# Expert rows of a routed network read in 256-byte pieces and turned by VectorE, in place of gathers turned by TensorE

## The chip, the cores and the metric

The kernel runs on one core of a Trainium2 chip. A core has five engines, each with an instruction queue of its own that is worked off in order: TensorE (PE; its weight loads are shown as PEld), VectorE (DVE), ScalarE (ACT), GpSimd (POOL) and SyncE (SP), which only issues transfers. All transfers run on the same 16 DMA engines. Matrix products land in PSUM, in banks that must be emptied before they are used again; everything else lies in SBUF (128 partitions) or in DRAM.

The metric is the time of one execution on the device, in microseconds. A few runs are made and their median is given; one more execution is recorded by the profiler.

## What is computed

A normalised linear attention, and then a layer of experts in which each token goes to one expert:

```python
kv  = einsum('bhsd,bhse->bhde', k, v)          # 8 batches, 8 heads, 576 tokens, 64 wide
out = einsum('bhsd,bhde->bhse', q, kv)
x   = out / sqrt(mean(out*out) + 1e-6) * g_norm  # rows: 4608 tokens x 512
...
expert = argmax(x @ w_gate)                    # one of 8
gate_w = softmax(x @ w_gate)[expert]
for e in range(8):
    h = relu(x[expert == e] @ w1[e])           # 512 -> 1024
    out[expert == e] = gate_w * (h @ w2[e])    # 1024 -> 512
```

The inputs q, k and v have 9.4 MB each and the expert weights 33.6 MB, all float32.

## The kernel before

**Attention.** A loop over b = 0 to 8 interleaves two things. For batch b it does the products k·v (`kv_mm`), the transposes of q (`t_mm`, a TensorE product with the identity, copied out by ACT) and `fold_mm`, which joins kv with the gate weights; `x_copy` brings the result to SBUF as `kvx`, one half by ACT and one half by VectorE. For the batch before, it runs four or five *tiles* of 128 tokens: `tile_step` multiplies q with kvx (`o_mm`, PSUM tag "O"), scales and casts the tile of before (`o_x`) and sums squares (`o_red`); `o_nrm` forms the root. The tiles are numbered (j, t), j = 0 to 3, t = 0 to 8. `load(b + 2, u)` is issued by SP as soon as the buffers of batch b are read, so loads run two batches ahead.

**Routing.** When some tiles are done (`chunks`: 9, 9, 3+6, 3+3+3), `route` is put on a list of jobs; `job()` is called twice a tile and runs it to its next `yield`. It finds each token's expert (`ohb`), counts with small TensorE products (`rps`) which row each token gets, and scatters the finished rows with 36 indirect transfers from POOL (line 743) into the DRAM array `x_slots`: 4608 rows for each of the 8 experts, a row being 512 float16, the gate's factor and the token's number (1032 bytes). The rows are built in `xrow`, with four buffers of three tiles each.

**Experts.** A row of work is a `Group`: three of 3 tiles (experts 0 to 2, whose first 384 rows are declared final once j = 0 to 2 are routed, `early_rows`), three of 2 tiles (the rest of experts 0 to 2), five of 5 tiles (experts 3 to 7). An expert has 640 slots; what is over goes to one more group of one tile (`SpillGroup`, with weights chosen at run time) and then to a loop of a count known only on the device (`LoopGroup`; with this input it has no round). For each group:

- `fetch` gathers the rows by indirect transfers of POOL, one for 128 rows (line 291), into a ring of three buffers `xl`. Slots that hold no row are left out by an index out of bounds; the ring was zeroed at the start.
- `xpose` turns each tile with four TensorE products with the identity into PSUM (`xps`, line 325), and VectorE writes it to `xsT` with the factor g_norm (line 328).
- `stage1(f)`, f = 0 to 7, is the first product (line 345, `hp`), with ACT's relu to `hT` (line 353).
- `stage2(k)` is the second product for 128 rows (line 361, `yp`), scaled by the gate on VectorE (line 366, `y`) and scattered to the output by POOL (line 369), with token numbers from `slot_ids`.

A generator, `ffn`, emits this a step at a time; `unit()` takes a step. The first steps are taken inside the last round of attention (b = 8, two after each tile from n = 3 on), one after each routing job, and the rest after it. The transposes of the next group are emitted between the stage 2 tiles of the present one, and the fetch of group r+2 at f = 0 of group r (the three early ones right after `early_rows`).

**Weights.** `w_load` (SP, lines 206 and 210) brings 512 KB into one of four staging buffers, `w_cast` (VectorE, line 220) turns it to float16; `w_step` does both, and is called from b = 6 on.

**Order.** The instructions of each engine run in the order in which the code emits them (`manual_schedule`). Waits between engines and between accesses to the same memory, `x_slots` and the output among it, are added by the framework: a reader of rows waits for the scatters emitted before it, a scatter for the readers emitted before it. The loop behind the experts stands outside this block: its count is read at line 850 by every engine, and its header (line 854) makes the engines wait for each other.

## Time and profile before

| | us |
|---|---|
| median of 3 runs (351.76 to 354.26) | 353.55 |
| the profiled execution's own time | 330.94 |
| its span, first to last instruction | 329.2 |
| TensorE busy | 269.0 |
| VectorE busy | 183.4 |
| GpSimd busy | 137.6 |
| ScalarE busy | 119.9 |

The profiled execution was 22.6 us shorter than the median of the runs; its mean granted TensorE clock was 0.903.

The costliest groups of instructions that the text below speaks of (line, engine, operation, output from inputs, how often, then busy us and mean ns of one, then idle us of the engine before them and what ended it):

```profile
L345 PE MATMUL hp<-xsT,w1e 128*128 128x320 f16 (+2 forms) x512 | 76.6, 306 | 7.2 <-DVE xsT L328 6.3
L361 PE MATMUL yp<-w2e,hT 128*128 128x512 f16 x320 | 74.1, 379 | 0.3 <-DVE y L366 0.3
...
L743 POOL DMA_INDIRECT x_slots<-xrow,posi x36 | 35.7, 991 | 40.5 <-DVE xrow L739 15.5
...
L291 POOL DMA_INDIRECT xl<-x_slots,idxa x31 | 32.4, 1046 | 11.7 <-issue 7.0
...
L328 DVE TENSOR_SCALAR xsT<-xps,g 128x512 f16<-128x512 f16 x41 | 19.2, 477 | 12.9 <-PE xps L325 12.7
```

In the timeline the last attention product ends at 148.6 us, the first expert product starts at 153.1, TensorE runs without larger gaps from 167.4, and its last product ends at 320.0. The scatters into `x_slots` run from 56.6 to 170.1, the nine early gathers from 139.8 to 152.2.

### The profile page before, as it was taken

What the parts mean: (1) busy time and instruction counts of PE and PEld (TensorE: products, weight loads), DVE (VectorE), ACT (ScalarE), POOL (GpSimd) and SP (SyncE); (2) the same over time, 40 slices, a digit from 0 to 9 for tenths busy, and PEclk for the clock granted to TensorE, in tenths of its full rate; (3) what the DMA queues carried; (4) which work ended last, traced back from release to release, by engine and by line L of the source; (5) the groups of instructions that cost most, each with busy time, mean ns of one, the idle gap of its engine ahead of it and who ended that gap; (6) DMA issues with size and microseconds to landing.
All of it is one profiled execution on the core that took longest, in us unless ns stands there. A gap on an engine that the chain in (4) does not pass through costs nothing.

```text
span 329.2 us, 7247 instructions
## 1 busy us (share of the span) xinstructions
PE 269.0 (82%) x2759; PEld 189.3 (58%) x2759; DVE 183.4 (56%) x433; ACT 119.9 (36%) x316; POOL 137.6 (42%) x147
## 2 busy tenths in 40 slices
PE   0699897689766977564979996989999999997980
PEld 0587776577656866462535563657565665645630
DVE  6205566346745368889184678344657658375040
ACT  1136564436543445322322431326142240602600
POOL 9100001720076004384675462777477656052041
PEclk9999997959995589555999998999999999999996
DMA  6999999997897016799589894667799999983021
GB/s 158 334 368 367 369 368 367 381 282 216 246 323 295 18 67 167 250 323 324 201 260 372 295 322 121 214 214 251 250 339 358 351 397 279 408 284 130 0 99 55
DMA packets 45395, 85.79 MB, mean 261 GB/s; under 512 B 6188, under 2 KB 22829, under 8 KB 45360
## 3 DMA queue, kind: packets, MB, share of 16 engines
q1 hardware_dynamic: 36736, 66.07, 59.9%
q0 software_dynamic: 6976, 18.96, 15.6%
q10 hardware_dynamic: 1648, 0.29, 0.5%
q8 instruction: 22, 0.36, 0.4%
q14 instruction: 13, 0.11, 0.1%
HBM read 71.77 MB, written 15.50 MB: 265 GB/s over the span
## 4 chain that ended last, share of the span: by engine, by line
PE 26%; issue 11%; DMA 9%; POOL 7%; DVE 5%; POOLq 1%; ACT 0%; DVEq 0%; ACTq 0%
PE hp L345 13%; PE yp L361 11%; DMA out_dram<-y,d_id 7%; POOL out_dram L369 4%; POOL xl L291 2%; DMA xl<-x_slots,idxe 2%; PE xps L325 1%; DVE y L366 1%; DMA x_slots<-xrow,posi 1%; POOL x_slots L743 1%; DVE w1e L220 1%; DVE xsT L328 0%; POOLq L888 0%; POOLq L854 0%; DVE w2e L220 0%
## 5 line engine op out<-in xcount | busy, mean ns | idle before, releaser
L353 ACT ACTIVATE hT<-hp 128x320 f16<-128x320 f32 (+3 forms) x136 | 53.6, 426 | 106.5 <-PE hp L345 105.9
L345 PE MATMUL hp<-xsT,w1e 128*128 128x320 f16 (+2 forms) x512 | 76.6, 306 | 7.2 <-DVE xsT L328 6.3
L361 PE MATMUL yp<-w2e,hT 128*128 128x512 f16 x320 | 74.1, 379 | 0.3 <-DVE y L366 0.3
L369 POOL DMA_INDIRECT out_dram<-y,idv x40 | 44.6, 1115 | 60.3 <-DVE y L366 49.3
L345 PEld LDWEIGHTS <-w1e 128*128 128x128 f16 x512 | 51.0, 100 | 32.1 <-issue 11.7
L651 PE MATMUL ops<-kvx,qT 64*128 64x72 f32 (+1 forms) x640 | 48.0, 310 | 10.5 <-DVE lhat L680 9.6
L743 POOL DMA_INDIRECT x_slots<-xrow,posi x36 | 35.7, 991 | 40.5 <-DVE xrow L739 15.5
L651 PEld LDWEIGHTS ops<-kvx,qT 64*128 64x128 f32 (+1 forms) x640 | 42.3, 215 | 15.0 <-issue 9.3
L361 PEld LDWEIGHTS <-hT 128*128 128x128 f16 x328 | 30.8, 98 | 31.6 <-issue 0.4
L366 DVE TENSOR_SCALAR y<-yp,xl 128x512 f32<-128x512 f32 x40 | 30.0, 750 | 33.6 <-PE yp L361 29.9
L664 DVE TENSOR_REDUCE ms<-sq 128x8 f32<-128x512 f32 x36 | 24.6, 685 | 25.1 <-ACT sq L660 25.0
L291 POOL DMA_INDIRECT xl<-x_slots,idxa x31 | 32.4, 1046 | 11.7 <-issue 7.0
L594 PE MATMUL kvps<-mk,mv 128*64 128x64 f32 x640 | 28.7, 258 | 9.4 <-DMA mv<-in_v_dram 9.1
L676 DVE TENSOR_TENSOR xrow<-ops,rs 128x512 f16<-128x512 f32 x36 | 24.7, 686 | 18.0 <-DMA x_slots<-xrow,posi 9.3
L660 ACT ACTIVATE sq<-ops 128x512 f32<-128x512 f32 x36 | 21.5, 598 | 31.9 <-PE ops L651 31.5
L594 PEld LDWEIGHTS kvps<-mk,mv 128*64 128x64 f32 x640 | 26.0, 168 | 11.8 <-issue 10.3
L710 POOL COPY xrow<-tokc 128x3 int32<-128x3 int32 x12 | 3.0, 253 | 64.3 <-DVE xrow L676 64.2
L582 PE MATMUL tps<-ctile,mq 128*128 128x128 f32 x144 | 26.9, 320 | 3.5 <-ACT qT L583 1.9
L220 DVE CAST w2e<-wst 128x1024 f16<-128x1024 f32 x32 | 22.3, 704 | 11.4 <-DMA wst<-in_moe_w_dram 11.4
L583 ACT COPY qT<-tps 128x384 f32<-128x384 f32 x48 | 21.9, 473 | 14.4 <-PE tps L582 14.4
L328 DVE TENSOR_SCALAR xsT<-xps,g 128x512 f16<-128x512 f16 x41 | 19.2, 477 | 12.9 <-PE xps L325 12.7
L220 DVE CAST w1e<-wst 128x1024 f16<-128x1024 f32 x32 | 21.6, 688 | 4.5 <-DMA wst<-in_moe_w_dram 4.5
(99 smaller groups left out, 184.1 us busy)
## 6 DMA issues: line engine op xcount, KB each, us to landing
wst<-in_moe_w_dram SPq DMA_DIRECT2D x64, 512.0 KB, 5.8
mq<-in_q_dram SPq DMA_DIRECT2D x16, 576.0 KB, 7.8
mk<-in_k_dram SPq DMA_DIRECT2D x16, 320.0 KB, 7.5
mv<-in_v_dram SPq DMA_DIRECT2D x16, 320.0 KB, 7.3
mk<-in_k_dram SPq DMA_DIRECT2D x16, 256.0 KB, 7.9
mv<-in_v_dram SPq DMA_DIRECT2D x16, 256.0 KB, 7.1
wsts<-in_moe_w_dram SPq DMA_DIRECT2D x8, 512.0 KB, 5.9
out_dram<-y,idv POOLq DMA_INDIRECT x40, 4.9
```

Of the source, the lines that this page charges most:

```text
L220: engine.tensor_copy(dst, st)
L291: nc.gpsimd.indirect_dma_start(out=self.xl[:, k, :], out_offset=None, in_=xs.ap(), in_offset=IndirectOffsetOnAxis(ap=idx[:, self.e, self.k ...
L345: nc.tensor.matmul(hp, self.w()[0][:, kk, f * 128 : (f + 1) * 128], self.xsT[:, kk, s : s + self.step], start=(kk == 0), stop=(kk == 3),)
L353: nc.scalar.activation(self.hT[:, f, s : s + self.step], hp, ACTF.Relu)
L361: nc.tensor.matmul(yp, self.hT[:, f, k * 128 : (k + 1) * 128], self.w()[1][:, f, :], start=(f == 0), stop=(f == 7),)
L366: nc.vector.tensor_scalar(y, yp, self.xl[:, k, D : D + 2].bitcast(F32), None, op0=ALU.mult)
L369: nc.gpsimd.indirect_dma_start(out=self.views(k), out_offset=IndirectOffsetOnAxis(ap=self.ids[:, k : k + 1], axis=0), in_=y, in_offset=Non ...
L582: nc.tensor.transpose(ps[:, c, :], src[:, 128 * m : 128 * m + 128], cv["ident"])
L594: nc.tensor.matmul(kvps[b][64 * y : 64 * y + 64, 2 * u + a, :], main["v", b, u][:, 2 * y + a, c, :], main["k", b, u][:, 2 * y + a, c, :], ...
L651: nc.tensor.matmul(ps[p0 : p0 + 64 * n, y, o0 : o0 + 72], qT[b][hs, a, blk // 2 : blk // 2 + n, :].rearrange("d c p -> d (c p)"), kvx[b][h ...
L676: nc.vector.tensor_tensor(xr[:, 0:D].bitcast(F16).rearrange("p (a h d) -> p a h d", a=2, h=4), xv, _bc(rs2, 3, 64), op=ALU.mult,)
L743: nc.gpsimd.indirect_dma_start(out=xs_views[9 * j + t0 + t], out_offset=IndirectOffsetOnAxis(ap=posi[:, t : t + 1], axis=0), in_=xrow[j, ( ...
```

## The change

- `fetch` no longer gathers. SP reads the rows r0 to r0 + n of an expert as they lie, in four transfers of 256-byte pieces: piece i of each row goes to partition group i (32 partitions), 32 rows beside each other. A fifth transfer brings gate and token number (8 bytes a row, `gi`).
- One `nc.vector.transpose` for the whole group turns all 32x32 blocks, reading every fourth element (`xT`). The columns of a product are then 32 contiguous values, 256 bytes apart (`xcols`). The rows of w1 are loaded in an order that fits (4p + c), and g_norm is multiplied into w1 when it is cast (`g4`).
- Since slots without a row are read too, `clear_slots` writes zeros over the 640 slots of each expert, with SP transfers in b = 1 and b = 2.
- The fetch of groups 0 and 1 is emitted in b = 8 after its first tile, that of group r+2 at f = 7 of group r; the transpose of group r+1 at f = 4 of group r. Expert steps are taken after each tile of b = 8 from n = 1 on.
- `fold_mm` uses the PSUM tag "KV" instead of "T", stage 2 of the early groups "KV" instead of "O"; both halves of `kvx` are copied by ACT; `xrow` has six buffers; `route` has one more `yield` before its small products; in b = 6 four weight loads are emitted at once.
- The spill and loop groups keep their gather and their TensorE transposes, with the new order of columns.
- The loop's count is read by the engines in the group of expert 4, and the loop stands inside the block of hand-made order, after the last scatter.

```diff
+    g4 = P_const.tile([128, 4], F32, tag="g4")
+    for n in range(8):
+        nc.scalar.dma_start(g4[16 * n : 16 * n + 16], g_norm.rearrange("(a c) -> a c", c=4))
...
+    zero = P_wa.tile([128, F], F32, tag="wst", bufs=4, name="zero")
+    nc.gpsimd.memset(zero[0:80], 0.0)
+
+    def clear_slots(e):
+        nc.sync.dma_start(
+            xs.ap()[e * N : e * N + SLOTS].rearrange("(p m k) w -> p m (k w)", m=4, k=2),
+            _bc(zero[0:80, 0:ROW].bitcast(I16), 1, 4),
+        )
...
-            r0 = 128 * (2 * (n % 2) + n // 2)
-            nc.sync.dma_start(st, w1[r0 : r0 + 128, :])
+            nc.sync.dma_start(st, w1.rearrange("(p c) f -> c p f", c=4)[n])
...
+            if n < 4:
+                engine.tensor_scalar(dst, st, g4[:, n : n + 1], None, op0=ALU.mult)
+            else:
+                engine.tensor_copy(dst, st)
...
         def fetch(self):
-            idx = rows[self.table][0]
-            for k in range(self.K):
-                nc.gpsimd.indirect_dma_start(
...
+            r0 = self.e * N + 128 * self.k0
+            src = xs.ap()[r0 : r0 + self.n].rearrange("(g b) w -> b g w", b=32)
+            self.xl = self.pool().tile([128, self.n // 32, 128], I16, tag="xl", bufs=2, name="xl")
+            for i in range(4):
+                c0 = 128 * (2 * (i % 2) + i // 2)
+                nc.sync.dma_start(self.xl[32 * i : 32 * i + 32], src[:, :, c0 : c0 + 128])
+            self.gi = P_fe.tile([128, SLOT_TILES, 4], I16, tag="gi", bufs=3, name="gi")
+            nc.sync.dma_start(
+                self.gi[:, 0 : self.K],
+                xs.ap()[r0 : r0 + self.n, D:ROW].rearrange("(k p) w -> p k w", p=128),
+            )
+
+        def xpose(self):
+            g = self.n // 32
+            self.xT = self.pool().tile([128, g, 4, 32], I16, tag="xT", bufs=2, name="xT")
+            nc.vector.transpose(self.xT, self.xl.rearrange("p g (a c) -> p g c a", c=4))
+
+        def xcols(self, kk, s):
+            return self.xT[:, s // 32 : (s + self.step) // 32, kk, :].bitcast(F16)
...
-                        self.xsT[:, kk, s : s + self.step],
+                        self.xcols(kk, s),
...
+            if real == 0:
+                cur.xpose()
...
-                if f == 0 and 1 <= real and EARLY <= real + 2 < len(groups):
-                    groups[real + 2].fetch()
+                if f == 4 and 0 <= real < len(groups) - 1:
+                    groups[real + 1].xpose()
...
+                    n_more.append(
+                        nc.values_load(
...
+                if f == 7 and 0 <= real < len(groups) - 2:
+                    groups[real + 2].fetch()
...
-                PSA.tile([128, 4, 72], F32, tag="T", bufs=2, name=f"fold{b}{y}")
+                PSA.tile([128, 4, 72], F32, tag="KV", bufs=2, name=f"fold{b}{y}")
...
-            nc.vector.tensor_copy(kvx[b][:, 1], folds[b][1])
+            nc.scalar.copy(kvx[b][:, 1], folds[b][1])
...
-                    [128, 3, ROW], I16, tag="xrow", bufs=4, name=f"xrow{j}{t}"
+                    [128, 3, ROW], I16, tag="xrow", bufs=6, name=f"xrow{j}{t}"
...
+            yield
             ex = rt("ex", [128, T, 8])
...
+                            for e in ((), (0, 1, 2, 3), (4, 5, 6, 7), ())[min(b, 3)][x // 3 :: 2]:
+                                clear_slots(e)
...
-                for _ in range((0, 1, 1, 2)[max(b - 5, 0)]):
-                    w_step()
-                if b == B and n >= 3:
+                if b == 6 and n == 0:
+                    for _ in range(4):
+                        w_load(P_wa, 3)
+                elif b >= 6:
+                    for _ in range(2 if b == B else 1):
+                        w_step()
+                if b == B and n == 0:
+                    for i in range(2):
+                        groups[i].fetch()
+                if b == B and n >= 1:
...
-    manual.close()
-
-    n_more = nc.values_load(
...
-    with tc.For_i(0, n_more) as it:
+    with tc.For_i(0, n_more[0]) as it:
...
+    manual.close()
```

## The prediction

> **What bounds the kernel now.** I read the page's slices first, then busy time by stage, then the chain of waits, then the waits one by one.
>
> ```profile
> PE   0699897689766977564979996989999999997980
> PEclk9999997959995589555999998999999999999996
> DMA  6999999997897016799589894667799999983021
> ```
>
> Each digit is 8.2 us. DMA is full to slice 9; TensorE is full from slice 19 on; slices 12 to 18 are full of neither. By stage (us, then busy us of each engine, clock, DMA share, GB/s):
>
> ```profile
> 20.00:66.00 46.00, 38.81 (x737) 33.32 (x737) 23.75 (x56) 25.18 (x69) 7.81 (x11) 0.96 1.07 370
> 66.00:118.00 52.00, 42.26 (x616) 36.46 (x618) 27.88 (x74) 23.82 (x66) 14.17 (x19) 0.74 0.67 217
> ...
> 132.00:156.00 24.00, 13.91 (x128) 11.29 (x129) 21.23 (x63) 6.66 (x20) 12.80 (x13) 0.50 0.89 300
> 156.00:168.00 12.00, 9.13 (x55) 4.87 (x55) 5.12 (x19) 3.42 (x8) 8.05 (x10) 1.00 0.63 212
> ...
> 204.00:320.00 116.00, 113.17 (x761) 69.19 (x759) 60.61 (x111) 38.42 (x104) 61.63 (x57) 0.99 0.73 255
> ```
>
> So there are three regimes: loads bound the start (370 GB/s), latencies between engines the middle, TensorE alone the expert stage (113 of 116 us, full clock). In the chain of waits the expert stage is TensorE only, the transposes in line with the rest:
>
> ```profile
> 253.27 0.22 PE xps L325 x4
> 253.49 1.73 PE yp L361 x8
> ```
>
> The waits in the middle, and the end in the timeline:
>
> ```profile
> DVE kvx L623 <- PE fold L614: 15.8, 7, 11.2
> ...
> PE rps L720 <- DVE ohb L708: 12.0, 6, 2.8
> ...
> DVE xrow L676 <- DMA x_slots<-xrow,posi: 9.3, 2, 5.0
> ...
> DVE posi L734 <- DMA x_slots<-xrow,posi: 6.7, 1, 6.7
> ```
>
> ```profile
> 320.07 0.75 DVE L366 TENSOR_SCALAR y<-yp,xl 128x512 f32<-128x512 f32 x1 [0.97 <-PE yp L361]
> 325.20 0.98 POOL L369 DMA_INDIRECT out_dram<-y,idv  x1 [4.67 <-issue]
> ```
>
> The last y is ready at 320.8, but its scatter starts at 325.2: POOL first walks the loop's header (L850, L854).
>
> [...] No transpose of VectorE is in this trace, but the 512-element reduce (L664) takes 685 ns[...]. [...] The new reads step 8 bytes (VectorE) and take 64-byte runs (TensorE); no run here shows either.
>
> **Part by part**, against the profiled execution (330.9 us, span 329.2). The runs' median is 353.55, 22.6 more; the trace can't say why, so I carry the difference in us over, not the level.
>
> *Transposes off TensorE.* 160 xps matmuls go: 40 tiles by 0.22 us. The first group's three lie beside waits; 37 x 0.22 = **8 us** off the bounding engine. VectorE loses 40 xsT evictions (477 ns, 19.1 us) and gets 11 transposes[...]. VectorE is busy 61 of 116 us, so I charge nothing; the next group's transpose is issued at f = 4, with half of stage 1 and two to five 1.73 us tiles ahead of its reader. Queued behind it are a cast, the ids and the y evictions; a y needed 4 us later is covered. A transpose of over 6 us would hold y, then yp's two banks, then TensorE. The w1 cast with a scale stays at its 0.69 us form (the xsT and y lines are such scaled forms)[...]. Dropping the scaled eviction moves no arithmetic onto the path.
>
> *Reads moved from POOL to SP.* 40 gathers of about 1.05 us leave POOL (42 us; scatters no longer queue behind them). SP gets 5 issues a group, 55 in all; its longest present issues are 0.60 us, so 0.6 to 1 us each, 3 to 5 us a group, ahead of weight loads. A group lasts 11 to 19 us and SP then issues some 8 loads of 0.34 to 0.38 us: it fits. Price of a piece: the queues give
>
> ```profile
> q1 hardware_dynamic: 36736, 66.07, 59.9%
> ...
> q10 hardware_dynamic: 1648, 0.29, 0.5%
> ```
>
> which is 86 ns for 1.8 KB and 16 ns for 176 B on one engine of 16, so about 20 ns for 256 B: 20480 pieces are 25 us of all engines, the 5120 gate/id pieces (8 B) about 4, against some 17 for the rows of before. 12 us more, over 170 us at share 0.73 to 0.8: no cost. Bounds: 16 ns (saves nothing) and 50 ns (see rivals).
>
> *Clears.* 8 x 640 x 1032 B = 5.3 MB, at 370 GB/s **14 us**, put into the only stage where DMA is full, ahead of the loads of batches 3 to 5 on SP. Loads run two batches ahead, and the stage after has a third of DMA free (52 x 0.33 = 17 us). 0 to 10 us; I take +3. Scatters now also wait for clears: the first ones (56.6 us) slide to 65 or so, held by nothing since xrow has six buffers. The three POOL memsets (2.2 us each) that go were hidden; so are the new one and the eight small g4 loads on ACT's queue (8 x 0.6 us behind 4.8 us of others, over before the first copy at 14.1 us), and the index arithmetic that falls away.
>
> *Middle.* The extra yield lets ohb be ready before TensorE reaches rps (12.0 us in six waits, 7.5 of them in 60 to 135); xrow's buffers remove 9.3 us of VectorE waiting and the 7.1 us it causes at ops; kvx on ACT frees VectorE of 4.6 us of waits (the 11.2 is the first load) and costs ACT 8 x 0.39 us, ACT being half idle. Some 15 us are named; part returns as the next wait (folds now share the two KV banks with kvps), part to the full DMA. I take −8, between −15 and 0.
>
> *Turn into the experts.* From 148.6 (last attention matmul) to 167.4 TensorE does about 9 us of expert work. After: the first two reads are issued by SP behind two loads, when the scatters of j = 2 have landed (issue ends at 134.9, median 6.4 to land), so about 141; 5 x 0.8 us of issue and 3 to land give 147[...]. VectorE takes its queue in order: this transpose stands before o_x and the sums of the last three or four tiles, so it waits up to 8 us with attention behind it, and loads on SP wait likewise. Against that group 0's stage 1 fills TensorE inside attention, the early gathers (12.4 us of POOL) are gone, and the last scatters no longer wait for them until 157.9, which released posi's 6.7 us. −4, between −10 and +8.
>
> *Tail.* Scatter at 321.1 instead of 325.2 is −4.1; the header then runs after its landing, 1.4 us (322.9 to 324.3): −2.7, between −4 and 0. The count's register loads in mid-stage cost TensorE's queue 0.7 us and some semaphore waits: +1, 0 to 2. dyn_tables' 3.1 us hole stays.
>
> Sum: −8 + 3 − 8 − 4 − 2.7 + 1 = **−18.7**: profiled 312, median about **335**.
>
> **Rivals.** (1) *Given back at the turn and at the loads*: the transpose's wait (+8), clears (+10), the middle's gains eaten by DMA (0): −8 − 2.7 + 1 + 18 = +8, half of that happening gives 349 (343 to 361). For it: DMA share 1.07; against: only the first batches are tight. (2) *Slower: TensorE reading xT in 64-byte runs.* Stage 1 streams 168,000 columns, 5,250 runs of 32. The gain is gone at 18.7/5250 = 3.6 ns a run; at 8 ns the kernel takes 353.6 − 18.7 + 42 = 377. Nothing in the trace has such a stream[...]. (3) *Pieces at 50 ns*: 64 us instead of 25, and DMA fills the expert stage (share 0.73 plus some 31 of 116 us); weights come late, beyond that 1.3 us for each ns: 340 to 370. The 16 ns on q10 speak against it. (4) *The scheduler still puts the last scatter behind the header*: 338 instead of 335.
>
> **Numbers.** As summed (with 4) 0.68, alone 322 to 346; rival 1 0.18; rival 2 0.08; rival 3 0.06. Range 320 to 358: past 358 lie most of 2 and 3 and the edge of 1, below 320 the sum of all good ends. About 1% (350.0 to 357.1) is what a measurement can tell from no change. Faster 0.70, same 0.11, slower 0.19.
>
> **What would show it.** No xps but for the spill; hp per 64 matmuls still about 8.7 us (rival 2: more); [...] small-packet queue time near 20 ns a piece; no DVE wait on xl over 8 us, and only at the turn; TensorE full from about 150; batches 4 and 5 without long waits on mq, mk, mv; last scatter within 1 us of the last y. The forecast is wrong if hp slows, if weight casts wait on DMA in the expert stage, or if attention ends later than 148.6.

## The result and the profile after

The changed kernel takes 367.89 us in the median of four runs (365.88 to 373.02) against 352.69 (351.76 to 354.26) for the kernel before: a ratio of 1.0407 [1.0333, 1.0482], **slower**. 335 was forecast. The profiled execution has a span of 365.4 us.

One thing must be known to read what follows. In two of the later sets of runs (all runs with a_ or b_ in the name) the kernel before has a median of 327.7 and 329.4 us, in all other sets, the result's among them, one of 352.7 to 358.5. The sets ran on different chips, the last two (d_ and e_) on the same one; I speak of chips of the 328 and of the 353 kind, though that it is the chip which makes the difference is not shown. The execution shown above (329.2 us) is of the first kind. So ratios are formed within a set only, and stages are set against those of the same kind; **e_before**, below, is a profile of the kernel before on a chip of the 353 kind.

The slices of the page of the changed kernel, 9.1 us each:

```profile
PE   0699979573956899328699877979986989579930
PEclk9999978885585957657699998999998999989985
DMA  5999999999996353487977694758996989992020
```

Counted from 0, DMA stands at 9 through slice 11 (110 us); before it did so through slice 8 (74 us; the prediction's slice 9 stands at 7). TensorE, at 9 in most slices of the expert stage before, now drops to 8, 7 and less again and again there. By stage (us, then busy us of PE, PEld, DVE, ACT, POOL; clock; DMA share; GB/s):

```profile
66.00:130.00 64.00, 43.71 (x566) 36.24 (x565) 25.80 (x68) 22.87 (x64) 21.38 (x26) 0.72 0.88 302
...
145.00:170.00 25.00, 10.76 (x91) 7.49 (x89) 13.72 (x35) 5.43 (x16) 6.95 (x9) 0.59 0.70 210
225.00:341.00 116.00, 101.08 (x611) 59.44 (x609) 63.09 (x90) 37.27 (x101) 31.66 (x29) 0.96 0.80 259
341.00:366.00 25.00, 9.65 (x48) 4.42 (x46) 3.75 (x5) 1.50 (x4) 4.92 (x5) 0.75 0.13 50
```

The expert stage of e_before, the same columns:

```profile
225.00:341.00 116.00, 107.01 (x717) 64.67 (x715) 58.12 (x106) 35.89 (x98) 55.02 (x50) 0.99 0.67 239
```

Of 116 us in the expert stage TensorE works 101; before it worked 113, and 107 in e_before. The middle moves 302 GB/s where it moved 217. The groups and waits that answer to those shown of before:

```profile
L338 PE MATMUL hp<-xT,w1e 128*128 128x320 f16 (+2 forms) x512 | 79.0, 311 | 16.8 <-DVE xT L302 11.8
L354 PE MATMUL yp<-w2e,hT 128*128 128x512 f16 x320 | 75.3, 392 | 13.0 <-DVE y L359 13.0
...
L302 DVE STREAM_TRANSPOSE xT<-xl 128x2560 int16<-128x2560 int16 (+2 forms) x11 | 23.3, 2115 | 23.0 <-DMA xl<-x_slots 21.8
```

```profile
PE kvps L615 <- DMA mv<-in_v_dram: 14.2, 6, 8.1
...
PE yp L354 <- DVE y L359: 13.0, 5, 4.3
...
PE hp L338 <- DVE xT L302: 11.8, 3, 7.4
DVE w1e L228 <- DMA wst<-in_moe_w_dram: 10.5, 4, 4.6
```

In the first profile these were 9.1, 0.3, 6.3 and 4.5 us in total; in e_before 9.6, none, 8.1 and 3.0. Of the mv waits the very first load is 8.1 in the changed kernel and 8.9 and 9.1 in the two others. They show the places to look: loads of attention, the evictions of y, the turn, the weight loads.

I cut each execution into four stretches: to the last k·v product; from there to the last product of attention (the turn); to the last expert product; from the last y to the end (the tail). In us, with the 0.7 to 0.8 between the last product and the last y left out; the names are those of the runs below:

| kernel | to last k·v | turn | experts | tail | span |
|---|---|---|---|---|---|
| chips of the 328 kind | | | | | |
| before, shown above | 125.4 | 23.2 | 171.4 | 8.4 | 329.2 |
| before, again (b_same) | 127.5 | 23.3 | 171.8 | 8.5 | 331.9 |
| changed (a_same) | 133.7 | 35.4 | 171.3 | 13.9 | 355.1 |
| a_clear4 | 121.8 | 35.5 | 169.2 | 13.9 | 341.2 |
| a_turn | 130.0 | 32.9 | 177.9 | 13.9 | 355.5 |
| a_fpool | 130.5 | 36.5 | 164.1 | 9.0 | 340.9 |
| a_xsplit | 129.3 | 37.1 | 161.9 | 14.0 | 343.1 |
| chips of the 353 kind | | | | | |
| before (e_before) | 134.3 | 32.6 | 178.6 | 8.4 | 354.7 |
| changed, result | 141.1 | 39.2 | 170.4 | 14.0 | 365.4 |
| d_clear4 | 126.8 | 41.2 | 173.4 | 13.9 | 356.1 |
| d_noorder | 138.1 | 43.9 | 173.1 | 13.9 | 369.8 |
| d_all | 128.8 | 41.8 | 169.4 | 9.2 | 350.0 |
| d_late | 128.1 | 28.9 | 175.5 | 8.9 | 342.2 |
| e_best | 126.5 | 28.9 | 174.7 | 8.9 | 339.8 |

Against its partner the changed kernel loses 6.8 us up to the last k·v product, 6.6 in the turn and 5.6 in the tail, and gains 8.2 in the experts; on the other kind (a_same against b_same) it loses 6.2, 12.1 and 5.4 and gains 0.5.

Part of this is work that only moved across the cut. In the kernel before no expert product runs ahead of the last product of attention. In the changed kernel 24 do, 6.4 us of TensorE (the same in a_same):

```profile
165.68 2.72 PE L338 MATMUL hp<-xT,w1e 128*128 128x384 f16 x8 [7.36 <-DVE xT L302]
...
169.85 1.47 PE L338 MATMUL hp<-xT,w1e 128*128 128x384 f16 x8
...
172.85 0.81 PE L338 MATMUL hp<-xT,w1e 128*128 128x384 f16 x4
176.92 1.44 PE L338 MATMUL hp<-xT,w1e 128*128 128x384 f16 x4 [3.26 <-ACT hT L346]
178.29 1.99 PE L672 MATMUL ops<-kvx,qT 64*128 64x72 f32 x16
```

With these counted as experts, the turn loses 0.2 us on the result's kind of chip and 5.7 on the other, and the experts gain 1.8 and lose 5.9. The variants of the changed kernel below all have 24 such products, but for a_turn (8, 2.7 us) and d_late and e_best (none).

**How y comes late** is seen in one group of five tiles. First VectorE, then TensorE, then SP's queue, all from the timeline of the changed kernel:

```profile
267.36 0.75 DVE L228 TENSOR_SCALAR w1e<-wst,g 128x1024 f16<-128x1024 f32 x1 [4.30 <-DMA wst<-in_moe_w_dram]
269.19 0.75 DVE L228 TENSOR_SCALAR w1e<-wst,g 128x1024 f16<-128x1024 f32 x1 [1.08 <-DMA wst<-in_moe_w_dram]
...
272.62 2.85 DVE L302 STREAM_TRANSPOSE xT<-xl 128x2560 int16<-128x2560 int16 x1 [1.19 <-DMA wst<-in_moe_w_dram]
275.39 0.65 DVE L230 CAST w2e<-wst 128x1024 f16<-128x1024 f32 x1
...
276.64 0.74 DVE L359 TENSOR_SCALAR y<-yp,gi 128x512 f32<-128x512 f32 x1
```

```profile
270.36 3.62 PE L354 MATMUL yp<-w2e,hT 128*128 128x512 f16 x16
277.43 6.81 PE L354 MATMUL yp<-w2e,hT 128*128 128x512 f16 x23 [3.46 <-DVE y L359]
```

```profile
255.05 5.80 SPq L292 DMA_DIRECT2D xl<-x_slots  x4
260.89 0.60 SPq L294 DMA_DIRECT2D gi<-x_slots  x1
```

From the bottom up: four row reads hold SP for 5.8 us, and the weight loads stand behind them. The casts of those weights therefore wait in VectorE's queue (4.30 and 1.08 us), the transpose of 2.85 us stands behind the casts, and the first y behind the transpose. TensorE fills its two banks of yp by 273.98 and then stands for 3.46 us.

This is one of five such waits. At the first of them (3.41 us, at 211.94) the lump is made longer by the rows themselves: the transpose ahead of it stood 3.35 us for them.

```profile
207.99 1.25 DVE L302 STREAM_TRANSPOSE xT<-xl 128x1024 int16<-128x1024 int16 x1 [3.35 <-DMA xl<-x_slots]
```

Five transposes of the expert stage waited 2.9 to 5.1 us each for their rows; how much of this reached TensorE is not shown.

### The profile page after: what moved, and what is told of

Read it like the earlier page. It is cut to its first block, busy times and chain, and to the rows that moved or that the text cites. A ratio compares the mean times of both kernels' runs of the same rounds, so it can differ in the third digit from the quotient of the medians.

```text
span 365.4 us, 6862 instructions
## 1 busy us (share of the span) xinstructions
PE 275.1 (75%) x2599; PEld 187.5 (51%) x2599; DVE 181.7 (50%) x395; ACT 121.5 (33%) x324; POOL 87.4 (24%) x104
## 5 line engine op out<-in xcount | busy, mean ns | idle before, releaser
L338 PE MATMUL hp<-xT,w1e 128*128 128x320 f16 (+2 forms) x512 | 79.0, 311 | 16.8 <-DVE xT L302 11.8
L354 PEld LDWEIGHTS <-hT 128*128 128x128 f16 x328 | 32.9, 101 | 52.8 <-issue 19.2
L672 PE MATMUL ops<-kvx,qT 64*128 64x72 f32 (+1 forms) x640 | 52.5, 315 | 8.5 <-issue 5.4
L615 PE MATMUL kvps<-mk,mv 128*64 128x64 f32 x640 | 35.4, 273 | 30.3 <-DMA mv<-in_v_dram 14.2
L672 PEld LDWEIGHTS ops<-kvx,qT 64*128 64x128 f32 (+1 forms) x640 | 44.8, 217 | 16.9 <-issue 12.4
L615 PEld LDWEIGHTS kvps<-mk,mv 128*64 128x64 f32 x640 | 30.6, 181 | 35.0 <-issue 31.8
L359 DVE TENSOR_SCALAR y<-yp,gi 128x512 f32<-128x512 f32 x40 | 29.6, 747 | 23.9 <-PE yp L354 21.3
L302 DVE STREAM_TRANSPOSE xT<-xl 128x2560 int16<-128x2560 int16 (+2 forms) x11 | 23.3, 2115 | 23.0 <-DMA xl<-x_slots 21.8
L228 DVE TENSOR_SCALAR w1e<-wst,g 128x1024 f16<-128x1024 f32 x32 | 23.8, 755 | 14.8 <-DMA wst<-in_moe_w_dram 10.5
L697 DVE TENSOR_TENSOR xrow<-ops,rs 128x512 f16<-128x512 f32 x36 | 24.6, 684 | 10.7 <-ACT rs L690 8.1
L604 ACT COPY qT<-tps 128x384 f32<-128x384 f32 x48 | 22.4, 474 | 14.9 <-DMA mk<-in_k_dram 11.9
L603 PEld LDWEIGHTS tps<-ctile,mq 128*128 128x128 f32 x144 | 19.4, 171 | 6.9 <-ACT qT L604 3.3
L689 ACT ACTIVATE rs<-ms,epsb 128x8 f32<-128x8 f32 x36 | 10.8, 301 | 20.6 <-DVE ms L685 18.6
```

What stands on the lines that cost most here:

```text
L228: engine.tensor_scalar(dst, st, g4[:, n : n + 1], None, op0=ALU.mult)
L338: nc.tensor.matmul(hp.rearrange("p (g b) -> p g b", b=32), self.w()[0][:, kk, f * 128 : (f + 1) * 128], self.xcols(kk, s), start=(kk == 0) ...
L354: nc.tensor.matmul(yp, self.hT[:, f, k * 128 : (k + 1) * 128], self.w()[1][:, f, :], start=(f == 0), stop=(f == 7),)
L359: nc.vector.tensor_scalar(y, yp, self.gate(k), None, op0=ALU.mult)
L603: nc.tensor.transpose(ps[:, c, :], src[:, 128 * m : 128 * m + 128], cv["ident"])
L615: nc.tensor.matmul(kvps[b][64 * y : 64 * y + 64, 2 * u + a, :], main["v", b, u][:, 2 * y + a, c, :], main["k", b, u][:, 2 * y + a, c, :], ...
```

## The experiments

### The clears, the size of the pieces, the old end

**a_clear4** zeroes only the last 128 slots of an expert (the last 384 of expert 1): 1.3 MB instead of 5.3. With this input the slots between hold rows.

```diff
     def clear_slots(e):
+        n = 384 if e == 1 else 128
         nc.sync.dma_start(
-            xs.ap()[e * N : e * N + SLOTS]...
-            _bc(zero[0:80, 0:ROW].bitcast(I16), 1, 4),
+            xs.ap()[e * N + SLOTS - n : e * N + SLOTS]...
+            _bc(zero[0 : n // 8, 0:ROW].bitcast(I16), 1, 4),
```

> The changed kernel with a quarter of the clears (128 of 640 slots of each expert, 384 of expert 1; those that no token fills with this input): 1.3 MB in place of 5.3. If the clears delay the loads of batches 4 to 6 and these delay everything after, TensorE's waits on mv at 66 to 112 us go and the time falls by 8 to 12 us (ratio to before about 1.01). If the loads are late for another reason, or the delay is made up later, it falls by under 3 us.

Measured 341.56 us, 1.0448 [1.0341, 1.0556]; the unchanged kernel, on another chip of this kind, has 1.0807 (a_same, below). The last k·v product comes at 121.8 instead of 133.7 us. On the other kind of chip (d_clear4, below) the ratio is 0.9928 against 1.0407. Three quarters of the clears thus cost 3.6 to 4.8%, **12 to 17 us**. Both figures cross sets. Within a_clear4's own set, a_big and a_oldtail (below) have all the clears: their last k·v product comes at 134.0 and 131.5 us.

How, is seen on the chips of the 328 kind in TensorE's waits between 40 and 135 us. Here a_same, with all clears, and then a_clear4:

```profile
PE ops L672 <- DVE lhat L701: 12.9, 1, 12.9
PE kvps L615 <- DMA mv<-in_v_dram: 7.0, 5, 3.2
```

```profile
PE ops L673 <- DVE lhat L702: 9.3, 3, 6.8
PE kvps L616 <- DMA mv<-in_v_dram: 2.1, 2, 1.7
```

The loads of v are late, as one would think, but the larger wait is another. The timeline of a_same says what stood ahead of lhat in VectorE's queue, and what TensorE did meanwhile:

```profile
115.42 0.75 DVE L228 TENSOR_SCALAR w1e<-wst,g 128x1024 f16<-128x1024 f32 x1 [13.16 <-DMA wst<-in_moe_w_dram]
116.09 0.68 DVE L697 TENSOR_TENSOR xrow<-ops,rs 128x512 f16<-128x512 f32 x1
```

```profile
117.01 1.99 PE L672 MATMUL ops<-kvx,qT 64*128 64x72 f32 x16 [12.89 <-DVE lhat L701]
```

The first weight load is pushed back with all loads; its cast stands in VectorE's queue ahead of attention and stops it for 13.2 us (7.1 in a_clear4). Five of the 11.9 us are late v, some 4 this cast; the rest is not named by these waits. In the execution of the result, on the other kind of chip, this stop is not listed (no w1e cast waits over 4.6 us), so how the clears cost time there is not shown.

A third effect is seen on both kinds. By the code, a scatter into `x_slots` waits for the clears emitted before it. POOL's first scatter in e_before, in d_clear4 and in the changed kernel:

```profile
56.60 1.14 POOL L743 DMA_INDIRECT x_slots<-xrow,posi  x1 [7.83 <-DVE lhat L680]
```

```profile
64.92 1.13 POOL L766 DMA_INDIRECT x_slots<-xrow,posi  x1 [17.18 <-DMA mk<-in_k_dram]
```

```profile
76.98 1.13 POOL L765 DMA_INDIRECT x_slots<-xrow,posi  x1 [28.02 <-DMA mk<-in_k_dram]
```

The profile puts these waits down to loads that landed last. The forecast had 65 us.

**a_big** reads the same bytes in pieces of 1024 instead of 256 bytes (`rearrange("p (r q) c -> p r (q c)", q=4)` on the target, whole rows as source). Values reach other places, so the expert products are of other numbers.

> The changed kernel with each group's rows read in pieces of 1024 bytes in place of 256: a quarter of the pieces, the same bytes, issues, waits and instructions; the values reach other places, so the expert products are of other numbers. If the number of pieces holds SP (5.8 us for four issues) and so the weight loads behind them, the waits of casts on weights (10.5 us) and of TensorE on y (13 us) in the expert stage go, and the time falls by 8 to 12 us (ratio about 1.01). If it is the place of the fetch in SP's queue, or the traffic as such, it falls by under 3 us.

356.97 us, 1.0942 [1.0828, 1.1055], beside 356.26 of a_same (below) on another chip of this kind: nothing gained. SP's four issues of a group take 2.5 us instead of 5.75, yet the period of a group of five tiles stays (20.4 to 22.7 us), and so do the waits on y (13.1 us; 14.6 in a_same). Neither the count of pieces nor the length of SP's four issues is the cause by itself.

**a_oldtail** sets the loop and the reading of its count back outside the block, as in the kernel before. **b_same** is the kernel before, profiled again.

> The changed kernel with the end of the kernel before: count read behind the experts, loop outside the hand-made order, the small memset ahead of it. If moving the loop made the end longer (13.9 us from the last y to the end against 8.4 before), 4 to 6 us come back (ratio about 1.025). If the long end is chance or belongs to the machine, nothing changes (1.04).

> The kernel before, unchanged, profiled once more. The profiled execution of before was 22 us shorter than its runs. If that execution was an exception, this profile has a span near 350 us, and shows where the other 20 us lie; if the profiler itself shortens it, the span is again near 330.

a_oldtail: 361.04 us, 1.1044 [1.0892, 1.1195]. The old place of the loop does not bring back the old tail: 15.8 us, not 8.4. b_same: 329.76 us, stretches as in the first profile.

### The turn, the queue of the reads, the length of the transpose

These four ran in one set (kernel before 329.42 us). **a_same** is the changed kernel; **a_turn** begins the expert steps after the fourth of the last five tiles; **a_fpool** lets POOL issue the reads of all groups but the early ones; **a_xsplit** cuts the transpose into one for each 128 rows, put between the stage 2 tiles.

```diff
-                if b == B and n >= 1:
+                if b == B and n >= 3:                      # a_turn
...
+            queue = nc.gpsimd if self.table == "all" else nc.sync
-                nc.sync.dma_start(self.xl[...
+                queue.dma_start(self.xl[...                # a_fpool
...
-                if f == 4 and 0 <= real < len(groups) - 1:
-                    groups[real + 1].xpose()
...
             for k in range(cur.K):
                 cur.stage2(k)
...
+                while todo and len(todo) > max(cur.K - 2 - k, 0):
+                    nxt.turn(todo.pop(0))                  # a_xsplit
```

> The changed kernel once more, as the measure for the others of this call, since the kernel before took 352.7 us in one call and 327.7 in another. If the two kernels differ by a fixed sum, it stays 15 us above the kernel before; if the kernel before was held up in the first call by something that the changed one doesn't feel, it is 30 us above (about 358 where before takes 328).

> The changed kernel with the expert steps inside attention begun after the fourth tile of the last round, as in the kernel before, in place of the second; the first transpose then stands behind two more tiles' work on VectorE. If the transpose that waits for the first rows holds attention up (12 to 16 us more from the last kv product to the last attention product), that stretch falls by 6 to 12 us and the time by 4 to 10. If the stretch is bound by the arrival of the rows and the scatters behind them, the time stays within 3 us.

> The changed kernel with the reads of the groups from the fourth on issued by POOL in place of SP: the same pieces and traffic, but no weight load queues behind them. If it is SP's order that makes casts wait for weights and so y and TensorE wait on VectorE, the period of a five-tile group (20 to 22 us, 18.4 before) falls to 18 and the time by 8 to 14 us. If POOL's issue of 640 pieces takes longer than a group, rows come late and it is slower. If it is the place of the transpose on VectorE, the time falls by under 3 us.

> The changed kernel with each transpose cut into one of 128 rows a tile (some 0.7 us each), emitted between the second-stage tiles as the TensorE transposes were, in place of one of 2.8 us at the fifth step of the first stage. If the lump ahead of y on VectorE holds the second stage (waits of TensorE on y 13 us), these go and the time falls by 6 to 12 us. If late weights hold VectorE whatever the transpose is like, it falls by under 3 us.

a_same 356.26 us, 1.0807 [1.0637, 1.0976]; a_turn 354.25, 1.0817 [1.0720, 1.0913], no change: what the turn gave back the experts lost (177.9 against 171.3), 3.7 us of it the work that moves between the two. a_fpool 342.23, 1.0455 [1.0367, 1.0543]; a_xsplit 347.02, 1.0633 [1.0533, 1.0732]. The experts became 7.2 and 9.4 us shorter. The waits on y, for a_same, a_fpool and a_xsplit in that order (us in total, times, longest):

```profile
PE yp L354 <- DVE y L359: 14.6, 6, 4.7
```

```profile
PE yp L355 <- DVE y L360: 8.5, 3, 5.3
```

```profile
PE yp L358 <- DVE y L363: 2.9, 3, 1.4
```

Two links of the chain above are thus real, reads in SP's queue and the lump in VectorE's. Which part of a read on SP does it is open, since shorter issues alone gained nothing (a_big); and a_xsplit changes the place of the transposes together with their length. That a_fpool gains more in all than a_xsplit, 14 us, comes from its tail: 9.0 instead of 13.9.

### The edits of attention's order

**d_noorder** takes d_clear4 (the same kernel as a_clear4) and sets four edits back: folds under "T", half of `kvx` on VectorE, four `xrow` buffers, one `yield` less. **c_noorder** is the same kernel, in an earlier set.

> The quarter of the clears again, as the partner of the next run on one chip. Theory: 3 to 6% slower than the kernel before, as in its first run (1.045); it gives what the order edits are set against. Rival: on this chip the clears weigh less, and it is within 2% of the kernel before.

> The quarter of the clears with the order edits of attention undone, beside its partner. Theory: the edits of the middle do what the forecast said (-8): undone, the time is 4 to 10 us over the partner's and the last kv product comes 4 to 10 us later. Rival: within 3 us of the partner; then the 5.6% of the first run of this kernel is the chip's.

> The quarter of the clears, with the order edits of attention undone: folds under tag T, half of kvx on VectorE, four xrow buffers, one yield in route less. Theory (the -8 of the forecast for the middle was right in kind): slower than the quarter of the clears alone by 4 to 10 us, that is 346 to 352, the last kv product 4 to 8 us later than its 121.8. Rival: the order edits bring nothing because the wait passes to the next link: within 3 us of 341.6.

d_clear4: 356.15 us, 0.9928 [0.9884, 0.9972]; d_noorder: 371.41, 1.0413 [1.0333, 1.0493]; c_noorder: 371.36, 1.0558 [1.0391, 1.0725]. On this kind of chip and beside the other edits, the order edits are worth **some 15 to 17 us**, and 11.3 of them lie before the last k·v product; the four were not tried one by one. One kernel gives 1.0413 and 1.0558 here, on two chips of the same kind: that is how far ratios of different sets can be apart. In that stretch d_noorder has a wait that d_clear4 has not, the one for `xrow`'s buffers:

```profile
DVE xrow L698 <- DMA x_slots<-xrow,posi: 12.6, 1, 12.6
```

It ends at 75.7 us, after a first scatter that came at 66.7 instead of 56.6. In e_before no such wait is listed at all. So here the six buffers bridge a delay that comes with the change; that it comes from the clears is argued from the code.

### The tail and the number of POOL's transfers

**c_gipool** reads gate and token number by 40 small transfers of POOL instead of 11 of SP; the rows stay on SP.

```diff
-            nc.sync.dma_start(
-                self.gi[:, 0 : self.K],
+            for k in range(self.K):
+                nc.gpsimd.dma_start(
+                    self.gi[:, k], xs.ap()[r0 + 128 * k : r0 + 128 * k + 128, D:ROW]
```

> The changed kernel, with gate and token number read by 40 small transfers of POOL (one for 128 rows) in place of 11 of SP, so POOL issues 118 transfers, as in the kernel before, and the late row reads stay on SP. Theory: the length of POOL's closing drain goes with the number of transfers that POOL issued; the drain falls from 6.4 to 2 to 3.5 us, the loop header's wait from 1.74 to 0.4 to 0.7, the tail from 14 to about 9, and the time by 5 us at most. Rival: the drain is set by something else (what SP issued last, or the loop's place): it stays at 6.4 and the tail at 14.

362.45 us, 1.0284 [1.0132, 1.0435]. In the last scatter of the changed kernel the move of the loop did what it should: the last y ends at 351.4, and

```profile
351.72 0.98 POOL L362 DMA_INDIRECT out_dram<-y,idv  x1 [0.74 <-POOLq L875]
```

it starts 0.3 us later (4.4 in the kernel before). What comes behind it is in the raw records of the sequencers only: a semaphore step of POOL in the loop's header, and POOL's closing DRAIN.

| kernel | transfers of POOL | header's step, us | closing DRAIN, us | tail, us |
|---|---|---|---|---|
| before | 118 | 0.40 | 3.35 | 8.4 |
| changed | 78 | 1.74 | 6.44 | 14.0 |
| a_oldtail | 78 | 1.72 | 7.75 | 15.8 |
| a_fpool | 118 | 0.69 | 2.11 | 9.0 |
| c_gipool | 118 | 0.43 | 1.06 | 8.3 |
| c_allp | 133 | 0.87 | 2.85 | 9.8 |

In the two kernels with the loop in its old place the record of the drain begins just ahead of the last scatter and contains it; behind that scatter lie 2.2 us of it in the kernel before and 6.6 in a_oldtail. With 40 transfers more, far from the end and small, the drain falls to a sixth and the tail to 8.3 us. The tail hangs on what POOL issued before; by what rule stays open, since 118 transfers give three values and 133 one that is longer than two of these.

### All together

**c_all** and **d_all** join the quarter of the clears, the late reads by POOL and the cut transpose. **c_allp** has POOL issue the early reads too. **d_late** is d_all with no expert step before attention's last product (`n >= 5`). **e_best** is d_late with the transpose of the first group emitted after attention's last tile, ahead of the weight casts of that place. **e_before** is the kernel before on e_best's chip.

> The changed kernel with three edits at once: a quarter of the clears (only the last 128 slots of an expert, 384 of expert 1, are zeroed; the slots between hold rows or are dropped), the late groups' reads issued by POOL, and the transpose cut into pieces of 128 rows between the stage 2 tiles. Theory: clears (-15), SP's queue (-14) and the long transpose ahead of y (-9) are three causes, the last two sharing one wait in the expert stage; then the sum is -25 to -35 against the changed kernel on the same chip: 320 to 332, that is equal to the kernel before or up to 2% faster. In the trace TensorE's waits on y vanish, the group period falls from 21.5 to 19 us or less, the closing drain stays near 2 us. Rival: the three edits recover one and the same slack, or VectorE is the bound in any order: 338 to 342, no better than the best single edit.

> As the three edits at once, with the reads of the early groups issued by POOL too, so SP has nothing but loads and clears. Theory: the turn (35 us from the last kv product to the last attention product, 23 before) comes from SP's early reads with the weight loads queued behind them: the turn falls to 25 to 30 us and the time by 3 to 8 us against the three edits. Rival: the turn comes from the transpose waiting in VectorE's queue for rows that land no earlier from POOL: no change within 3 us, or worse by what the scatters of the last tiles lose behind POOL's reads.

> The three edits at once again (quarter of the clears, late reads by POOL, transpose in pieces), as the partner of the next run. Expected from its first run: 0.97 to 1.00 of the kernel before.

> The three edits at once, and no expert step before the last product of attention (in the changed kernel they begin after the second of the last five tiles). Theory: the 8 to 10 us gap of TensorE ahead of the first expert product is a wait for rows that must land whichever queue reads them, and it is doubled because attention products stand behind that product in TensorE's queue; with attention ahead of it, attention ends some 15 us earlier, the first expert product comes where it came (26 to 28 us after the last kv product), and the time falls by 4 to 9 us against its partner. Rival: the gap of TensorE is only moved (as when the steps began with the fourth tile, no change): within 3 us of its partner.

> As the three edits with no expert step before attention's last product, and the transpose of group 0 emitted in the last round of attention, ahead of the weight casts that stood before it in VectorE's queue. Theory: in the run without this edit TensorE stood still for 9.7 us between the last attention product and the first expert product, with the rows of group 0 landed some 10 us before VectorE came to them, behind four weight casts and the sums of attention; moved ahead, the gap falls to 1 to 4 us, the first expert product comes within 4 us of the last attention product, and the kernel is 4 to 7% faster than the kernel before on the same chip (its partner without the edit was at 0.969). Rival: the next wait in line (weights of expert 0, or attention's end held up by the transpose) takes the gap's place: 0.965 to 0.975.

> The kernel before, with a profile on the same chip, so that its stages can be set against the run above: last kv product at 125 to 128 us on every chip, and if this chip gives 350 and not 328, theory: the difference is in the expert stage and the turn at a lower granted clock. Rival: it lies in the loads of attention.

c_all 348.93 us, 0.9884 [0.9740, 1.0029]; d_all 350.94, 0.9869 [0.9785, 0.9954]; c_allp 351.04, 0.9882 [0.9829, 0.9936]: which queue makes the early reads doesn't matter for the time. c_all had been expected at 320 to 332. On this kind of chip the two expert edits and the tail together bring only 5 us over d_clear4, 4.7 of them in the tail and 4.0 in the experts, with 2.6 lost earlier; the 7 and 9 us of the other kind are not repeated.

d_late 344.36 us, **0.9694 [0.9624, 0.9763]**, 6.6 us under d_all. Not as I thought, though: I expected the first expert product where it was. TensorE of d_all and of d_late, before that product:

```profile
145.28 1.98 PE L686 MATMUL ops<-kvx,qT 64*128 64x72 f32 x16 [1.21 <-DVE lhat L715]
155.88 2.72 PE L344 MATMUL hp<-xT,w1e 128*128 128x384 f16 x8 [8.62 <-DVE xT L306]
```

```profile
155.71 1.31 PE L686 MATMUL ops<-kvx,qT 64*128 64x72 f32 x10
166.76 2.71 PE L344 MATMUL hp<-xT,w1e 128*128 128x384 f16 x8 [9.74 <-DVE xT L306]
```

The gap is as long as before, and the first expert product comes 11 us later. But attention ends at 157.0 instead of 170.6, and the experts, no longer mixed with it, take 165.7 us from first to last product instead of 184.1.

e_best: 341.71 us (338.09 to 345.90, six runs) beside 358.50 (349.08 to 363.27, ten runs); no interval was formed for this pair, but the two ranges don't touch, and the shortest run of the kernel before is 2.2% above e_best's median. The gap fell only to 7.7 us, not to 1 to 4: two casts further up in VectorE's queue still wait for loads that stand behind the early reads on SP:

```profile
156.77 0.69 DVE L231 CAST w2e<-wst 128x1024 f16<-128x1024 f32 x1 [3.00 <-DMA wst<-in_moe_w_dram]
158.06 0.72 DVE L231 CAST w2e<-wst 128x1024 f16<-128x1024 f32 x1 [0.60 <-DMA wst<-in_moe_w_dram]
```

e_before (362.37 us) gives the kernel before 9 us more to the last k·v product, 9 in the turn and 7 in the experts than the first profile. So the difference of the chips is not in the experts and the turn alone.

## Why the prediction was wrong

The sign was wrong. Step by step, in the prediction's order:

| step | forecast, us | what the runs showed |
|---|---|---|
| transposes off TensorE | −8 | right in kind, but hidden: −7 to −8 in two kernels without the lumps, on one chip |
| VectorE's transposes | "charge nothing" | wrong: the experts 9.4 us shorter with the transpose cut up, on one kind of chip |
| reads moved to SP | "it fits" | wrong: 7.2 us in the experts, on one kind of chip |
| price of a piece | 20 ns, no cost | right: some 20 ns at most, by an estimate from the queues (last section), and fewer pieces gained nothing |
| clears | +3 (0 to 10) | three quarters of them cost 12 to 17 |
| middle | −8 (−15 to 0) | −15 to −17, beside clears |
| turn | −4 (−10 to +8) | +6.6, +12.1 on the other kind; 6.4 of each is expert work that moved there |
| tail | −2.7 (−4 to 0) | +5.6 |
| count read in mid-stage | +1 (0 to 2) | not measured alone |

**The clears are the largest miss.** The step read that "the stage after has a third of DMA free" and let the loads catch up there. The stage did take them up: 302 GB/s at a share of 0.88, from 217 at 0.67. But each k·v product needs its own batch (5 us more of waits for v in a_same than with a quarter of the clears), and the first weight cast, at the head of VectorE's queue, turned a late load into a stop of attention (13.2 us against 7.1); both are from chips of the 328 kind. The forecast asked what the DMA could carry, not who waits for a late load. Up to the last k·v product, the steps from e_before over d_noorder and d_clear4 to the changed kernel are +3.8 (a quarter of the clears and what else of the change falls there), −11.3 (order edits), +14.3 (the rest of the clears), in sum +6.8. The rest of the clears is 4.0 MB, 10.7 us at the prediction's 370 GB/s, and it cost 11.9 to 14.3 us up to there. So the free share of the next stage took nothing off; the whole price was the low end.

**The middle was right in sign and past the far end of its range.** Waits that the forecast named did go: TensorE's rps on ohb falls from 16.2 us in e_before to 2.4, and the wait for `xrow` is gone. But the latter (12.6 us in d_noorder, 9.3 in the first profile) is not listed in e_before, so on this kind of chip part of the −15 to −17 takes back what the change itself seems to bring.

**The two steps costed at nothing** failed in their cover. How long VectorE's transposes would take was my estimate, since no view of before shows one; the longest takes 2.85 us. "A y needed 4 us later is covered" was measured against two to five tiles of 1.73 us; but with two banks for yp the cover is two tiles, 3.6 us, and the transpose (2.85) with two casts is more (272.62 to 276.64). And "it fits" compared SP's busy time with the length of a group, where what counts is what stands behind what in SP's queue: with the reads on POOL the experts are 7.2 us shorter. The chain shown above has weight loads behind reads, late casts, and VectorE's queue passing that on; since shorter issues gained nothing (a_big), how much of the 7.2 goes that way is open. The bound that I named for the transpose (6 us) was too high, since it left out the casts (0.65 to 0.75 us each).

The −8 appears where the lumps are gone. From the first expert product to the last: 174.0 us in e_before, 165.7 in d_late, 167.1 in e_best, all on one chip. TensorE's transposes in this stretch fall from 152 to the 4 of the spill group, while its idle time hardly changes (12.8 us in e_before, 13.7 in d_late). On the other kind of chip the kernel before needs only 166.9 for the stretch, and no kernel without both lumps ran there, so the −8 rests on these three profiles.

**The turn** was forecast as "up to 8 us with attention behind it" at its bad end. The gap of TensorE ahead of the first expert product is 7.4 us (10.3 in a_same) with attention products queued behind; 2.8 us in the first profile. With the 6.4 us of moved work taken out, the turn is 0.2 us longer on the result's kind of chip and 5.7 on the other, where −4 was forecast. (The forecast's landing of the first rows, 141 with 4 and 3 us, sums to 148, not 147.) A start with the fourth tile (a_turn) leaves the gap at 9.5 us. Early reads by POOL shorten it to 5.5 (c_allp; 8.4 in c_all), but the time stays. Putting attention first does pay (d_late).

**The tail** gained the forecast 4.1 us, and lost them: the header, once run before the scatter, now stands behind it, 5.4 us from the end of that instruction to the closing drain where 1.4 was assumed, and 6.4 us of drain follow where 2.2 lay behind the scatter before. That the drain goes with what POOL issued (6.44 us behind 78 transfers, 1.06 behind 118 in c_gipool) was in no view of the kernel before.

**The rivals.** Rival 1, the gains given back at the turn and at the loads, named two of the real places, with 343 to 361 as its times; the tail and y take it beyond. Rivals 2, 3 and 4 are out: 64 matmuls of hp take 8.86 us (8.69 to 8.86 before), a 256-byte piece some 20 ns at most by the estimate in the last section, and the last scatter starts 0.3 us after the last y. The 0.08 of rival 2 was my estimate alone, as no view of before shows such a stream. Of what should have shown the forecast wrong, two signs came: casts of weights waiting on DMA (10.5 us; 3.0 in e_before) and attention's end later than 148.6 (180.3). Part of the second is there without the change: e_before ends attention at 166.9.

## What to carry to other kernels

Free DMA time in a later stage doesn't pay for transfers put into a full one, if each later step waits for its own load: take the whole price (here 4.0 MB, 10.7 us at 370 GB/s, cost 11.9 to 14.3 us up to the last k·v product). An instruction that is "beside other work" must be measured against the buffers of whatever stands behind it in its queue (here two PSUM banks, 3.6 us), and a transfer moved to another queue against what stands behind it there (7.2 us of the experts between a_same and a_fpool). When work moves across the border between two stages, count it before comparing the stages (here 6.4 us). When several changes come together, a real gain (here 8 us of TensorE) can stay hidden until the lumps are taken out, so find those by single edits and then put them together.

## What the runs showed of the hardware

- The block transpose takes 2842 ns for 2560 two-byte elements, 1776 for 1536 and 1242 for 1024 in the changed kernel, with a stride of four elements in the source: 1.04 ns an element and some 0.18 us. For 512 this line gives 0.71 us; c_all took 699 ns.
- TensorE reads a moving operand in runs of 64 bytes, 256 bytes apart, at the old speed: a matmul of 320 columns takes 299 ns in the mean, as in the kernel before, and 64 of them 8.86 us (8.69 to 8.86 before). Those of 256 columns take 296 ns (295 before), those of 384 have a mean of 366 (341), but 32 of them in a row take 5.69 us in both kernels.
- A 256-byte piece takes some 20 ns of one DMA engine at most, by an estimate. Queue q1 has 697 us more of packet time in a_same (67.8% of 16 engines over 355.1 us) than in the first profile (59.9% over 329.2). Three quarters of the clears are 1,920 packets and 211 us of it (a_clear4 has 66.7% over 341.2 us), so all of them are 281. The other 416 us lie in 20,480 such pieces, with nothing taken off for the 5,120 pieces of 8 bytes.
- POOL's closing drain lasts 1.06 to 3.35 us in the kernels with 118 or 133 transfers of POOL (before, a_fpool, c_gipool, c_allp) and 6.44 or 7.75 in those with 78 (changed, a_oldtail).
- On the chips where the kernel before takes 353 us or more, ACT and VectorE stop in the middle of attention for something that this core's records don't show ("remote", 20 to 44 us in total by profile); in the profiles of the other kind no such wait is listed. Of e_before:

```profile
DVE kvx L623 <- remote: 15.8, 2, 9.6
...
ACT kvx L622 <- remote: 13.2, 2, 9.0
```

What ends these waits is open; it was not tried.
